# One change to an attention and two-layer network kernel: own raw buffers for the fourth head pair of the first group, and other engines allowed for casts, copies and scalings

## The chip, the cores and the metric

The kernel runs on one core of a Trainium2 chip. The metric is the device time of one execution in microseconds (us). The kernel before takes 654.95 us, the median of three runs (654.11 to 655.26). A core has five engines with a program each, that wait for one another by semaphores: TensorE (PE in the profile, its weight loads PEld), VectorE (DVE), ScalarE (ACT), GpSimd (POOL) and SyncE (SP), which here issues nearly all DMAs. An engine works off its program in order: whatever waits, holds up all that stands behind it on that engine.

## The reference

Attention over 4 batches of 8 heads, 768 positions and 64 numbers a head. A query sees the first 8 positions and the last 96 before it; scores are lowered by a slope times the distance. Its output, 3072 rows of 512, goes through a network of two layers:

```python
scores = scale * q @ k.T + bias           # bias = -slope[h] * distance
a = exp(scores - max) ; a = a / (sum(a) + 1e-9)
x = (a @ v) as (B*S, H*D)                 # 3072 x 512
h = x @ w_in                              # 512 x 2048
g = where(h > 0, h, exp(min(h, 0)) - 1)
out = g @ w_out                           # 2048 x 512
```

The weights come as 64-bit floats and the result must be nearly exact, so the two large products are each made of three: every factor is split into a high part (rounded to fp32r) and the rest, and high*high, high*low and low*high are summed.

## The kernel before, in words

**Tiling.** The 3072 rows are cut into 12 groups of 256 rows. In a group the 8 heads are handled as 4 pairs (two heads fill the 128 partitions). The hidden size of 2048 is cut into 16 chunks `fc` of 128, each with a tile of the first weights (`w0`) and of the second (`w1`).

**The stages.** Groups 0, 1 and 2 use the method of `pair` with `rows` set, and `pair32`: a pair's raw data is loaded into `rqv` (queries and values) and `rk` (keys), the queries are multiplied by the scale in place (`scaled`), PE makes the scores `s` (`s L691`), VectorE adds the distance table and takes the row's extreme (L647), ScalarE takes the exponential (L649), the sums are inverted on VectorE (L662, L663), the probabilities `pr` are multiplied by the inverse (`norm`; four tiles a pair), PE transposes them into `t` (L708), the transposed are copied out of PSUM into `pt`, and PE multiplies by the values into `pv` (L725). `pv` is copied as high part into `xh`, and the rest is subtracted. The copies, casts and subtractions of all stages go through the helpers `copy` and `minus`, so their lines in the profile are L336 (ScalarE), L338 (VectorE or GpSimd copies) and L344 (differences).

Beside that, `weight` turns each weight tile into two fp32r parts: a load of 512 KB (`bits`), four passes over 128x512 on ScalarE and VectorE (L433 to L442) that make an fp32 `g` of it, a cast of `g` to the high part, and a subtraction for the low part. The network for groups 0 to 2 (`moe`: `h L803`, `o L763`) runs over chunks 0 to 4 first, for all three groups, then 5 to 9, then 10 to 15. From group 3 on another scheme (`moe7`) with sums of weights (`combos`) takes over, with its TensorE order written out (`seq`).

**What sets the order.** Every operation is given to a planner with the engines that it may run on and a cost for each, with the tiles that it reads and writes and a due time. `Plan.order` then plays the program through with these costs and fixes for every operation the engine and the place in that engine's program; so a cost that is changed moves everything behind it. An alternative is a triple: engine, cost in ns, and whether it is held to take the port that VectorE and GpSimd share. Buffers are slots with names. The raw data of a pair in groups 0 to 2 lies in one of three slots (`rqv0`, `w015`, `w115`; keys `rk0`, `w014`, `w114`; the `w` names are space that the last weights use later). A pair's load thus waits until the pair three places earlier has finished its product with the values.

In `run` some weight loads are afterwards put together, right behind the load of the queries and values of group 1's second pair: those of the chunks named in `ASKED`. In the gaps that the planner foresees early on, `warm` and `fill_gap` put products that nobody reads (`none<-fill`, `o<-w 128x128`), which keep TensorE busy.

Of the kernel before, what the change touches and what calls it, by code (L numbers as in the profile page):

```python
# [16 lines left out]
P = 128  # L17
# [4 lines left out]
HK = WN // 2  # L22
NT = 2
W = NT * P
BIG = float(2 ** 100)

HI, LO = 0, 1
# [232 lines left out]
def act(n, psum=False, extra=0.0):  # L260
    return (("ACT", (55 if psum else 97) + 0.834 * n + extra, False),)


def dve(n, fast=False, port=False):
    return (("DVE", (75 + 0.521 * n) if fast else (70 + 1.042 * n), fast or port),)


def pool(n, two=True):
    return (("POOL", (30 + 2.58 * n) if two else (50 + 1.1 * n), True),)


def sp():
# [3 lines left out]
class Kernel:  # L276
# [136 lines left out]
    def weight(self, which, fc, due, after):  # L413
        nc, p, DM = self.nc, self.plan, self.DM
        tag = f"w{which}{fc}"
        bits = self.sb(tag, "bits", [P, 2 * DM], I32)
        g = self.sb("io", "g", [P, DM], I32)
        w = self.sb(tag, f"w{which}", [P, 2, DM], F32R)
        src = (self.w_in, self.w_out)[which][fc].bitcast(I32)
        words = lambda: bits.t.rearrange("p (n w) -> p n w", w=2)  # L420
        low, high = lambda: words()[:, :, 0], lambda: words()[:, :, 1]
        gf = lambda: g.t.bitcast(F32)

        def fetch(e):
            nc.sync.dma_start(bits.t, src)
            while self.values:
                self.values.pop(0)()

        load = p.add(sp(), fetch, writes=[bits], due=due - 9000, after=after, nbytes=P * DM * 8)
        if fc in self.ASKED:  # L430
            self.asked.append(load)
        if which in self.ABS:
            p.add((("ACT", 575.0, False),), lambda e: nc.scalar.activation(gf(), high().bitcast(F32), AF.Abs), [bits], [g], due - 6000)  # L433
            p.add(dve(DM, True), lambda e: nc.vector.tensor_scalar(gf(), gf(), F64_MIN, F64_MAX, ALU.max, ALU.min), [g], [g], due - 5500)
        else:
            p.add(dve(DM, port=True), lambda e: nc.vector.tensor_scalar(
                gf(), high().bitcast(F32), F64_MIN, F64_MAX, ALU.abs_max, ALU.min), [bits], [g], due - 5500)
        p.add(dve(DM, True), lambda e: nc.vector.tensor_scalar(g.t, g.t, 3, 0x3FFFFFFF, ALU.logical_shift_left, ALU.bitwise_and),
              [g], [g], due - 5000)
        p.add(dve(DM, port=True), lambda e: nc.vector.scalar_tensor_tensor(g.t, high(), -0x40000000, g.t, ALU.bitwise_and, ALU.bitwise_or),  # L440
              [bits, g], [g], due - 4500)
        p.add(dve(DM, port=True), lambda e: nc.vector.scalar_tensor_tensor(g.t, low(), 29, g.t, ALU.logical_shift_right, ALU.bitwise_or),  # L442
              [bits, g], [g], due - 4000)
        p.add(act(DM), lambda e: self.copy(e, w.t[:, HI], gf()), [g], [w], due - 3000)
        p.add((pool(DM) if due < 90000.0 else ()) + dve(DM, port=True), lambda e: self.minus(e, w.t[:, LO], gf(), w.t[:, HI]),
              [g, w], [w], due - 2000)
        if which == 0 or fc < self.NF7:
            cols = slice(0, DM) if which == 0 else slice(DM // 2, DM)
            self.stores[which, fc] = p.add(sp(), lambda e: nc.sync.dma_start(self.kept[which][fc], w.t.bitcast(F32)[:, :, cols]), [w],
                                           due=due + self.KEEP, nbytes=P * DM * 8 // (1 + which), floor=self.KEEP)  # L450
        return w
# [30 lines left out]
    def pair(self, b, gi, hp, xh, xl, due, ahead, step, X):  # L482
        nc, p = self.nc, self.plan
# [4 lines left out]
        rows = X.get("rows")  # L488
        nq, nk = W, KW
        rqv = self.sb("rqv", "rqv", [P, nq + VC if rows else nq], slots=X.get("rqv"))  # L490
        rv = rqv if rows else self.sb("rv", "rv", [P, VC])
        rk = self.sb("rk", "rk", [P, nk], slots=X.get("rk"))
        src = self.qkv[b, gi, hp]
        early = due - 9000 if rows else ahead - 9000
        if b == gi == 0 and hp < 3:

            vs, ks = slice(nq + P, nq + VC), slice(k0, nk)
# [26 lines left out]
        if rows:  # L524

            if "held" in X:
                self.loads += loads
            p.add((() if b == gi == 0 and hp < 3 else act(W) + dve(W, True)) + pool(W, False),
                  lambda e: self.scaled(e, q32(), q32(), sc), [rqv], [rqv], due - 9000)
            pv = self.bank("pv", "pv", [P, NT, P], X.get("pv"))  # L530
            self.pair32(b, hp, t0, q32, k32, v32, rqv, rk, pv, due, step, X)
            pvs = lambda: pv.t.rearrange("p i w -> p (i w)")
            p.add(act(W, True) + dve(W), lambda e: self.copy(e, xh.t[:, HI, hp], pvs()), [pv], [xh], due + 700)
            p.add(dve(W), lambda e: self.minus(e, xh.t[:, LO, hp], pvs(), xh.t[:, HI, hp]), [pv, xh], [xl], due + 800)
            if "held" in X:
                self.held += [o for v in (rqv, rk) for o in v.readers]
            return
# [139 lines left out]
    def pair32(self, b, hp, t0, q32, k32, v32, rqv, rk, pv, due, step, X):  # L677


        nc, p = self.nc, self.plan  # L680
# [5 lines left out]
        d = due - step  # L686
# [13 lines left out]
        for j in range(2):  # L700
            for i, x in enumerate(tiles):
                self.norm(prs[j][i], x[2], st, j * NT + i, d - 3000 + 2 * j + i, True)
            tp = self.bank("t", "t", [P, NT, 2, P], X.get("t"))

            def transposes(e, j=j, tp=tp):
                for i, (_, _, _, a0, kr, blocks) in enumerate(tiles):
                    for a in range(a0, 2):
                        nc.tensor.transpose(tp.t[:kr, i, a], prs[j][i].t[:, blocks[a]], self.ident.t)  # L708

            n = sum(2 - x[3] for x in tiles)  # L710
            p.add((("PE", 20 + 108.0 * n, False),), transposes, prs[j], [tp], d - 2500 + j)
            pt = self.sb("pt", "pt", [P, NT, 2, P], slots=X.get("pt"))
            pts.append(pt)
            if t0:
                p.add(act(NT * 2 * P, True) + dve(NT * 2 * P), lambda e, pt=pt, tp=tp: self.copy(e, pt.t[:HK], tp.t[:HK]), [tp], [pt], d - 2000 + j)
            else:
                for i, (_, _, _, a0, kr, _) in enumerate(tiles):
                    p.add(act((2 - a0) * P, True) + dve((2 - a0) * P), lambda e, pt=pt, tp=tp, i=i, a0=a0, kr=kr: self.copy(
                        e, pt.t[:kr, i, a0:], tp.t[:kr, i, a0:]), [tp], [pt], d - 2000 + j)

        def values(e):
# [213 lines left out]
    def build(self):  # L935
# [11 lines left out]
        for n, f0, f1 in segs:  # L947
            start.setdefault(n, at)
            d, at0 = {}, at
# [11 lines left out]
        for n, (b, gi) in enumerate(groups):  # L961
# [6 lines left out]
            for hp in range(self.NP):  # L968
                d = lo + (hp + 1) * (hi - lo) / self.NP
                X_ = self.EARLY[min(n, len(self.EARLY) - 1)]  # L970
                if n > self.GS:
                    X_ = {"seven": True}
                ahead = last - 2500
                if n > self.GS:
                    ahead = start[self.GS] + self.PERIOD * (4 * (n - self.GS - 1) + hp - 2) + self.VISIT
# [40 lines left out]
    AFTER = 2 * PERIOD  # L1016
    PASSES, SINCE = 2, 195000.0
    GS, KEEP, COMBO = 3, 100000.0, 0.0
    LATE, ASKED = 11, (2, 3, 4)
    ABS = (0, 1)  # L1020
    LINE = 32
    PLACE = {"w015": (80, 0), "w014": (0, 48), "w012": (80, 0), "w013": (0, 48), "xh0": (160, 0), "xh1": (32, 0), "gg0": (80, 0), "gg1": (0, 0)}
# [293 lines left out]
```

## Time and profile before

| What | us |
|---|---|
| median of three runs | 654.95 |
| the profiled execution | 655.49 |
| its span, first to last instruction | 653.70 |
| TensorE busy in the span | 642.0 (98%) |
| VectorE busy | 522.0 (80%) |
| ScalarE busy | 478.4 (73%) |
| GpSimd busy | 27.1 (4%) |

The profiled execution is one run; its span leaves out 1.8 us around the program. Busy time of TensorE counts also the products that nobody reads, and each product's modelled end reaches into the next one. In the chain of waits, each piece is what the end of the program hung on at that time, followed backwards.

### The profile page before, as it was taken

To read this page: it belongs to the slowest core of one execution; us is meant where nothing else is said; L and a number is where in the kernel's file an instruction comes from. 1 tells how busy PE (TensorE), PEld (TensorE's weight loads), DVE (VectorE), ACT (ScalarE), POOL (GpSimd) and SP (SyncE) were. 2 spreads that over 40 slices of the span, in tenths; PEclk is the share of its full clock that TensorE was granted. 3 is DMA by queue.
4 is the path that set the end of the run, shared out by engine and by line. 5 is a ranking of instruction groups with operands and counts; after the bars stand their busy time and mean duration, and the time that the engine had idled before them with its cause. 6 is when DMAs were issued, how large, how long until landed. Compare 5 with 4: busy or idle time off the path is not lost.

```text
span 653.7 us, 15985 instructions
## 1 busy us (share of the span) xinstructions
PE 642.0 (98%) x5950; PEld 599.4 (92%) x5950; DVE 522.0 (80%) x1520; ACT 478.4 (73%) x1244; POOL 27.1 (4%) x54
## 2 busy tenths in 40 slices
PE   8899999999999999999999999999999999999996
PEld 6677888888888999999999999999999999999996
DVE  7999999999999867866877886876777778766655
ACT  6898888765778777776777777776777777774442
POOL 3152100000000000000000000000000000000000
PEclk9999999999999999999999999999999999999999
DMA  8835996810237567667756756766775675574661
GB/s 273 293 118 193 383 379 223 301 61 17 71 114 255 198 212 255 224 196 224 264 187 214 272 180 221 253 218 202 230 262 181 223 282 189 178 255 169 209 211 36
DMA packets 52373, 137.71 MB, mean 211 GB/s; under 512 B 5698, under 2 KB 19010, under 8 KB 52290
## 3 DMA queue, kind: packets, MB, share of 16 engines
q1 hardware_dynamic: 52000, 136.37, 61.6%
q8 instruction: 48, 0.79, 0.5%
q14 instruction: 35, 0.29, 0.1%
q10 hardware_dynamic: 290, 0.26, 0.1%
HBM read 119.84 MB, written 16.78 MB: 209 GB/s over the span
## 4 chain that ended last, share of the span: by engine, by line
PE 90%; DVE 4%; ACT 2%; DMA 2%; issue 1%; POOL 0%; DVEq 0%; POOLq 0%; SPq 0%
PE h L803 39%; PE a L880 26%; PE o L763 9%; PE pv L614 4%; PE s L556 3%; PE t L576 3%; PE s L691 2%; DMA rqv<-in_qkv_dram 2%; PE pv L725 2%; PE t L708 2%; ACT pr L649 1%; DVE g L464 1%; PE none L1084 0%; DVE gl L344 0%; ACT pt L336 0%
## 5 line engine op out<-in xcount | busy, mean ns | idle before, releaser
L803 PE MATMUL h<-xh,w0s 128*128 128x256 f32 x1728 | 203.1, 276 | 0.0
L803 PEld LDWEIGHTS h<-xh,w0s 128*128 128x128 f32 x1728 | 199.5, 188 | 0.1
L880 PE MATMUL a<-w,gg 128*128 128x256 f32 x864 | 143.7, 277 | 0.3 <-DVE xh L344 0.3
L336 ACT CAST gg<-z 128x384 fp32r<-128x384 f32 (+1 forms) x144 | 81.4, 566 | 69.7 <-DVE z L735 29.7
L735 DVE SCALAR_TENSOR_TENSOR z<-z,h 128x512 f32<-128x512 f32 x72 | 49.5, 688 | 92.9 <-ACT z L734 86.0
L880 PEld LDWEIGHTS a<-w,gg 128*128 128x128 f32 x864 | 120.4, 188 | 0.6 <-DVE xh L344 0.5
L649 ACT ACTIVATE pr<-pr,nmax 128x232 f32<-128x232 f32 (+1 forms) x192 | 90.0, 471 | 9.2 <-DVE nmax L647 8.9
L344 DVE TENSOR_TENSOR gg<-z,gg 128x512 fp32r<-128x512 f32 (+1 forms) x144 | 84.9, 618 | 7.2 <-ACT gg L336 6.6
L803 PEld LDWEIGHTS h<-xh,w 128*128 128x128 f32 x576 | 81.7, 188 | 8.8 <-issue 1.1
L803 PE MATMUL h<-xh,w 128*128 128x256 f32 x576 | 86.7, 282 | 0.1
L835 DVE TENSOR_TENSOR z<-z 128x128 f32<-128x128 f32 (+1 forms) x216 | 72.0, 333 | 5.2
L880 PE MATMUL a<-ta,gg 128*128 128x256 f32 x432 | 72.2, 276 | 0.0
L647 DVE CUSTOM_DVE_ANT_0 pr<-s,tab 128x232 f32<-128x232 f32 (+1 forms) x192 | 63.5, 374 | 5.6 <-PE s L556 5.6
L733 ACT ACTIVATE z<-h 128x512 f32<-128x512 f32 x72 | 43.0, 597 | 33.2 <-PE h L803 32.9
L763 PE MATMUL o<-w,gh 128*128 128x512 f32 x192 | 59.8, 403 | 0.8 <-ACT gh L336 0.4
L880 PEld LDWEIGHTS a<-ta,gg 128*128 128x128 f32 x432 | 59.6, 188 | 0.0
L880 PE MATMUL a<-tb,gg 128*128 128x256 f32 x216 | 50.0, 294 | 0.0
L734 ACT ACTIVATE z<-z 128x512 f32<-128x512 f32 x72 | 45.5, 632 | 1.8
L633 ACT ACTIVATE pr<-pr,st 128x232 f32<-128x232 f32 (+1 forms) x90 | 38.9, 469 | 9.6 <-DVE st L669 7.3
L880 PEld LDWEIGHTS a<-tb,gg 128*128 128x128 f32 x216 | 34.4, 188 | 3.8 <-issue 0.2
L763 PEld LDWEIGHTS o<-w,gh 128*128 128x128 f32 x192 | 31.8, 188 | 5.8 <-ACT gh L336 1.1
L649 ACT ACTIVATION_READ_ACCUMULATOR pr<-pr,nmax 128x1 f32 x192 | 36.8, 192 | 0.0
(126 smaller groups left out, 916.4 us busy)
## 6 DMA issues: line engine op xcount, KB each, us to landing
w0s<-kept SPq DMA_DIRECT2D x144, 512.0 KB, 5.0
rk<-in_qkv_dram SPq DMA_DIRECT2D x45, 184.0 KB, 2.8
bits<-in_w_in_dram SPq DMA_DIRECT2D x16, 512.0 KB, 6.5
bits<-in_w_out_dram SPq DMA_DIRECT2D x16, 512.0 KB, 9.4
kept<-w SPq DMA_DIRECT2D x16, 512.0 KB, 4.4
rv<-in_qkv_dram SPq DMA_DIRECT2D x32, 256.0 KB, 3.6
rqv<-in_qkv_dram SPq DMA_DIRECT2D x13, 384.0 KB, 3.5
rqv<-in_qkv_dram SPq DMA_DIRECT2D x34, 128.0 KB, 3.8
```

Of the source, the lines that this page charges most:

```text
L336: self.nc.scalar.copy(out, x)
L344: self.on(e).tensor_tensor(out, x, y, ALU.subtract)
L633: self.nc.scalar.activation(out, x, AF.Copy, scale=sc)
L647: p.add((("DVE", 158 + 1.042 * n, False),), lambda e: nc.vector.tensor_tensor_reduce(pr.t[:, lo:], st_()[:, lo:], tab, -(2.0 ** -(h + 1)), ...
L649: p.add(act(n, extra=200), lambda e: nc.scalar.activation(pr.t[:, lo:], pr.t[:, lo:], AF.Exp, bias=nm, scale=-1.0, accum_out=st.t[:, 0, i: ...
L733: p.add(act(n, True), lambda e: nc.scalar.activation(out(), hx(), AF.Relu, scale=-1.0), [h], [ex], due)
L734: p.add(act(n), lambda e: nc.scalar.activation(out(), out(), AF.Exp, scale=-1.0), [ex], [ex], due)
L735: p.add(dve(n), lambda e: nc.vector.scalar_tensor_tensor(out(), out(), -1.0, hx(), ALU.add, ALU.max), [h, ex], [ex], due)
L763: nc.tensor.matmul(acc[i].t, g.t[:, i * P:(i + 1) * P], w2.t[:, s], start=fc == f0 and n == 0 and s == HI, stop=fc == f1 - 1 and n == 1)
L803: self.nc.tensor.matmul(hx(), w1.t[:, s, cc * P:(cc + 1) * P], xh.t[:, x, cc], start=n == 0 and cc == 0, stop=n == 2 and cc == self.NCC - 1)
L835: tt = lambda e, out, x, y, op: self.on(e).tensor_tensor(out, x, y, op)
L880: nc.tensor.matmul(of[i].t[:, j], gg.t[:, x, g], w(s), start=first and x == s == 0 and (n in (0, 2, 4, 6) or final and n == 5), stop=last ...
```

## The change

There are five edits. The fourth pair of the first group gets raw buffers of its own (`ks0` for queries and values, `qs0` for keys, space that later stages use), and its loads get a later due time (25000 where 11000 stood). Of the weight loads that `run` puts together only chunk 2's stay (`ASKED`). The cast of a weight's high part may go to GpSimd. The copies of the transposed probabilities in groups 0 to 3 may go to ScalarE alone (before also to VectorE), and the scaling of the queries of all but the first three pairs to ScalarE or GpSimd (before also to VectorE). And GpSimd's costs for operations with one input are others, and those are no longer held to take the shared port.

```diff
 def pool(n, two=True):
-    return (("POOL", (30 + 2.58 * n) if two else (50 + 1.1 * n), True),)
+    return (("POOL", (30 + 2.58 * n) if two else (30 + 1.85 * n), two),)
+
+
+def cast(n):
+    return (("POOL", 50 + 1.14 * n, False),)
...
-        p.add(act(DM), lambda e: self.copy(e, w.t[:, HI], gf()), [g], [w], due - 3000)
+        p.add(act(DM) + cast(DM), lambda e: self.copy(e, w.t[:, HI], gf()), [g], [w], due - 3000)
...
-        early = due - 9000 if rows else ahead - 9000
+        early = X.get("asked", due - 9000) if rows else ahead - 9000
...
-            p.add((() if b == gi == 0 and hp < 3 else act(W) + dve(W, True)) + pool(W, False),
+            p.add((() if b == gi == 0 and hp < 3 else act(W)) + pool(W, False),
                   lambda e: self.scaled(e, q32(), q32(), sc), [rqv], [rqv], due - 9000)
...
-                p.add(act(NT * 2 * P, True) + dve(NT * 2 * P), lambda e, pt=pt, tp=tp: self.copy(e, pt.t[:HK], tp.t[:HK]), [tp], [pt], d - 2000 + j)
+                p.add(act(NT * 2 * P, True), lambda e, pt=pt, tp=tp: self.copy(e, pt.t[:HK], tp.t[:HK]), [tp], [pt], d - 2000 + j)
...
-                    p.add(act((2 - a0) * P, True) + dve((2 - a0) * P), lambda e, pt=pt, tp=tp, i=i, a0=a0, kr=kr: self.copy(
+                    p.add(act((2 - a0) * P, True), lambda e, pt=pt, tp=tp, i=i, a0=a0, kr=kr: self.copy(
...
+                if n == 0 and hp == 3:
+                    X_ = dict(X_, rqv=["ks0"], rk=["qs0"], asked=25000.0)
...
-    LATE, ASKED = 11, (2, 3, 4)
+    LATE, ASKED = 11, (2,)
```

Counted over the whole program, 20 of the 32 casts of weights move from ScalarE to GpSimd; 8 copies of transposed probabilities move from VectorE to ScalarE; of the scalings of queries 6 leave VectorE and 1 leaves ScalarE, all to GpSimd; of the products of probabilities with the inverse sum 9 more go to VectorE, 4 fewer to ScalarE and 5 fewer to GpSimd; and one `gl` difference goes from GpSimd to VectorE.

SyncE's program at its start, before. `rqv_302` and `rk_201` are the raw data of group 0's fourth pair, `rqv_348` and `rk_213` of group 1's first, `rqv_390` and `rk_234` of its second; `bits` are weights.

```order
L425 DMA bits_186<-in_w_in_dram 128x1024
L425 DMA bits_188<-in_w_out_dram 128x1024
L425 DMA bits_191<-in_w_out_dram 128x1024
L517 DMA rk_201<-in_qkv_dram 128x368
L517 DMA rk_213<-in_qkv_dram 128x368
L517 DMA rk_234<-in_qkv_dram 128x368
L516 DMA rqv_302<-in_qkv_dram 128x768
L516 DMA rqv_348<-in_qkv_dram 128x768
L517 DMA rk_371<-in_qkv_dram 128x368
L516 DMA rqv_390<-in_qkv_dram 128x768
```

The same place now, where the fourth pair's data are `rqv_188` and `rk_191`, and those of group 1's first two pairs `rqv_303`, `rk_195` and `rqv_351`, `rk_220`:

```order
L429 DMA bits_186<-in_w_in_dram 128x1024
L520 DMA rqv_188<-in_qkv_dram 128x768
L521 DMA rk_191<-in_qkv_dram 128x368
L521 DMA rk_195<-in_qkv_dram 128x368
L429 DMA bits_209<-in_w_out_dram 128x1024
L429 DMA bits_214<-in_w_out_dram 128x1024
L521 DMA rk_220<-in_qkv_dram 128x368
L521 DMA rk_238<-in_qkv_dram 128x368
L520 DMA rqv_303<-in_qkv_dram 128x768
L520 DMA rqv_351<-in_qkv_dram 128x768
```

The fourth pair's loads moved ahead of two weight loads and no longer stand behind a buffer that must come free; the loads of group 1's first two pairs have moved up one place in the ring of three slots.

TensorE's program before, from the transposes of the second pair (`t_296`, `t_304`) on; `pv_330` is that pair's product with the values:

```order
L708 MATMUL t_296<-ident,pr_215 128x128
L708 MATMUL t_296<-ident,pr_218 116x128 x2
L708 MATMUL t_304<-ident,pr_228 128x128
L708 MATMUL t_304<-ident,pr_230 116x128 x2
L1084 MATMUL none<-fill 128x512 x4
L725 MATMUL pv_330<-pt_310,rqv_165 64x128
L725 MATMUL pv_330<-pt_316,rqv_165 64x128
```

And now, where the second pair's transposes are `t_299` and `t_308`, and `s_313`, `s_314` are the fourth pair's scores:

```order
L712 MATMUL t_299<-ident,pr_217 128x128
L712 MATMUL t_299<-ident,pr_222 116x128 x2
L712 MATMUL t_308<-ident,pr_232 128x128
L712 MATMUL t_308<-ident,pr_235 116x128 x2
L695 MATMUL s_313<-rk_191,rqv_188 128x128
L695 MATMUL s_314<-rk_191,rqv_188 128x128
L695 MATMUL s_313<-rk_191,rqv_188 128x232
L695 MATMUL s_314<-rk_191,rqv_188 128x232
L1090 MATMUL none<-fill 128x512
```

The fourth pair's scores, which before stood behind the third pair's transposes, now stand in front of the second pair's product with the values, in the place of three of four products that nobody reads.

GpSimd's program before, at the products of probabilities with the inverse sums of the second (`pr_215`, `pr_218`), third (`pr_262`, `pr_275`) and fourth pair (`pr_381` to `pr_404`) and the next one:

```order
L637 TENSOR_SCALAR pr_215<-pr_215,st_226 128x128
L637 TENSOR_SCALAR pr_218<-pr_218,st_226 128x232
L637 TENSOR_SCALAR pr_262<-pr_262,st_267 128x128
L637 TENSOR_SCALAR pr_275<-pr_275,st_267 128x128
L637 TENSOR_SCALAR pr_381<-pr_381,st_385 128x128
L637 TENSOR_SCALAR pr_387<-pr_387,st_385 128x128
L637 TENSOR_SCALAR pr_404<-pr_404,st_385 128x232
L637 TENSOR_SCALAR pr_426<-pr_426,st_445 128x232
```

And now (`pr_232` is the second pair's, `pr_264` and `pr_294` the third's, `pr_328` and `pr_371` the fourth's):

```order
L641 TENSOR_SCALAR rqv_188<-rqv_188,scale 128x256
L641 TENSOR_SCALAR pr_232<-pr_232,st_230 128x128
L342 CAST w_99_330<-g_242 128x512
L641 TENSOR_SCALAR pr_264<-pr_264,st_291 128x128
L641 TENSOR_SCALAR pr_294<-pr_294,st_291 128x128
L641 TENSOR_SCALAR rqv_303<-rqv_303,scale 128x256
L641 TENSOR_SCALAR rqv_351<-rqv_351,scale 128x256
L641 TENSOR_SCALAR pr_328<-pr_328,st_342 128x128
L641 TENSOR_SCALAR pr_371<-pr_371,st_342 128x232
L342 CAST w_105_468<-g_373 128x512
L348 TENSOR_TENSOR w_105_468<-g_373,w_105_468 128x512
```

Scalings of queries and casts of weights now stand between the products with the inverse sums; those of the fourth pair stand behind the scalings of two pairs of group 1. From the first transposes of the later scheme (L576) on, TensorE's programs are the same row for row.

## Rows read from the trace of the kernel before

**Rows 1.** Page, its head.

```profile
span 653.7 us, 15985 instructions
```

**Rows 2.** Busy time by engine in four stretches: PE, PEld, DVE, ACT, POOL; clock, DMA, GB/s.

```profile
0.00:10.00 10.00, 8.45 (x35) 6.70 (x36) 7.18 (x46) 5.24 (x17) 3.68 (x15) 1.00 0.77 243
10.00:62.00 52.00, 47.81 (x381) 36.62 (x380) 49.66 (x170) 46.52 (x148) 16.20 (x25) 1.00 0.61 206
62.00:197.00 135.00, 134.35 (x934) 116.98 (x932) 131.53 (x349) 103.92 (x283) 7.18 (x15) 1.00 0.54 198
197.00:654.00 457.00, 451.41 (x4606) 439.13 (x4604) 333.60 (x958) 322.71 (x799) 0.00 (x0) 1.00 0.64 214
```

**Rows 3.** The chain that ended last, 10 to 62 us: start, us, what.

```profile
19.52 4.09 DMA rqv<-in_qkv_dram
...
23.63 0.51 ACT rqv L633
...
26.72 0.47 ACT w L336
...
33.68 0.30 ACT gh L336
...
46.73 3.60 DMA rqv<-in_qkv_dram
...
50.35 0.35 DVE rqv L635
...
57.22 0.35 DVE rqv L635
```

**Rows 4.** Timeline, SyncE and TensorE, 13 to 27 us: start, us, engine, line, operation.

```profile
13.01 0.33 SPq L516 DMA_DIRECT2D rqv<-in_qkv_dram  x1
...
13.67 0.76 PE L708 MATMUL t<-ident,pr 128*116 128x128 f32 x5 [0.47 <-POOL pr L637]
...
17.31 0.89 PE L691 MATMUL s<-rk,rqv 64*128 64x128 f32 x8
...
26.87 1.07 PE L803 MATMUL h<-xh,w 128*128 128x256 f32 x4
```

**Rows 5.** VectorE's groups by shape, 0 to 62 us: busy, mean ns, idle before.

```profile
L635 DVE TENSOR_SCALAR pr<-pr,st 128x232 f32<-128x232 f32 x8 | 3.0, 392 | 0.0
L635 DVE TENSOR_SCALAR rqv<-rqv,scale 128x256 f32<-128x256 f32 x5 | 2.5, 503 | 0.3 <-DMA rqv<-in_qkv_dram 0.3
...
L338 DVE COPY pt<-t 116x512 f32<-116x512 f32 x2 | 1.4, 678 | 0.0
...
L338 DVE COPY pt<-t 116x256 f32<-116x256 f32 x2 | 0.8, 425 | 0.2 <-ACT pt L336 0.2
```

**Rows 6.** ScalarE's groups by shape, 0 to 62 us.

```profile
L336 ACT CAST w<-g 128x512 fp32r<-128x512 f32 x9 | 5.6, 618 | 0.0
L336 ACT COPY pt<-t 116x512 f32<-116x512 f32 x9 | 5.2, 577 | 0.3 <-PE t L708 0.2
L633 ACT ACTIVATE pr<-pr,st 128x232 f32<-128x232 f32 x11 | 5.2, 489 | 1.2 <-DVE st L663 1.2
```

**Rows 7.** GpSimd's groups by shape, 0 to 62 us.

```profile
L637 POOL TENSOR_SCALAR pr<-pr,st 128x232 f32<-128x232 f32 x13 | 7.1, 553 | 21.3 <-DVE st L663 17.4 <-ACT w L336 4.0
L344 POOL TENSOR_TENSOR w<-g,w 128x512 fp32r<-128x512 f32 x4 | 5.2, 1296 | 3.2 <-ACT w L336 3.0
...
L637 POOL TENSOR_SCALAR rqv<-rqv,scale 128x256 f32<-128x256 f32 x5 | 2.4, 482 | 4.2 <-DMA rqv<-in_qkv_dram 3.4 <-DVE n_six L401 0.8
```

**Rows 8.** Timeline, GpSimd and VectorE side by side, near 12.5 and 43 us.

```profile
12.18 1.44 POOL L637 TENSOR_SCALAR pr<-pr,st 128x128 f32<-128x128 f32 x2 [2.35 <-DVE st L663]
...
12.69 0.68 DVE L440 SCALAR_TENSOR_TENSOR g<-bits,g 128x512 int32<-128x512 int32 x1
...
42.89 1.27 POOL L344 TENSOR_TENSOR w<-g,w 128x512 fp32r<-128x512 f32 x1
...
43.23 1.09 DVE L635 TENSOR_SCALAR rqv<-rqv,scale 128x256 f32<-128x256 f32 x1
```

## The prediction, made before the result was known

> **What bounds the kernel now.** I read the busy times by stretch first, to see where TensorE can gain at all. From 62 to 197 us it is busy 134.35 of 135 us, and from 197 us on only the tail leaves gaps [rows 2]; its program is the same row for row from the later scheme's first transposes on. In those stretches the sum of TensorE's work is the time, and the change takes no useful product away. Before 62 us it is different: TensorE is busy 8.45 of 10 and 47.81 of 52 us, and part of that are products that nobody reads [rows 2]. So the gain or loss is made in the first 62 of 653.7 us [rows 1].
>
> The second view is the chain of waits in that time. It hangs on other engines in turn: on the load of raw data at 19.52 (4.09 us), on ScalarE from 23.63 to 33.98, then for 12.7 us on TensorE itself, on another load at 46.73 (3.60 us), on VectorE from 50.35 to at least 57.57 [rows 3]. The third view, the busy times again, shows why: between 10 and 62 us VectorE is busy 49.66 of 52 us and ScalarE 46.52, GpSimd only 16.20 [rows 2]. The stretch is bound by VectorE and ScalarE nearly alike, with the ring of three raw buffers in between.
>
> **The sum, part by part.** The profiled execution took 655.49 us, 0.54 above the median of the runs shown, with a span of 653.7 and 1.8 around it; differences are made against it and put on the median.
>
> *The fourth pair's own buffers.* Before, its queries and values were asked for at 13.01, when the first pair's product with the values had freed a slot, and its scores began at 17.31 [rows 4]. Now eleven loads stand ahead of it, one of them on ScalarE's queue: three each of 131, 135 and 197 KB and two weights of 524 KB, together 2.4 MB, and 3.0 MB with its own two. At 243 GB/s [rows 2] they have landed at 12.4 us, with the 1 us of the start 13.4. The scaling takes 0.48 [rows 7]. The place in TensorE's program comes up when the second pair's transposes end, before at 13.67 + 0.76 = 14.43 [rows 4]. So the scores can begin 2.8 us earlier. The two loads that freed-up places bring forward are those of group 1's first two pairs: the one at 19.52 in the chain waited for the third pair's product and now waits for the second's, about one pair's work earlier, 2 to 3 us.
>
> Part of it is given back. On GpSimd two of the fourth pair's products with the inverse sums now stand behind the scaling of `rqv_351`. Its load leaves when the second pair's product is done, at about 16.5, lands up to 4.09 later [rows 3], and after two more small operations and the scaling the products end near 21.9; without that queue they could have ended nearer 20.6. I take 1.5 us of the 2.8 as lasting. Ends: 0.5 (the queue takes nearly all) and 2.8.
>
> *ScalarE.* I count its program up to its eighth first pass over `h` (L733), which before falls near the stretch's end. It loses 9 of 11 casts of weights at 0.618 = 5.6 us [rows 6], two scalings at 0.51 = 1.0 [rows 3] and two products with the inverse at 0.489 = 1.0 [rows 6]. It gains two copies of 116x512 at 0.577 = 1.2 [rows 6] and five smaller operations, taken at 0.4 each, 2.0. Net 4.4 us less, or 9.5% of its 46.5 busy us [rows 2]. The chain hangs on it for 10.3 us [rows 3], so 1.0 us. Bounds: nothing, if those 10 us turn out to be waits for others, and 1.7, if two casts and a scaling that stand in the stretch go (0.5 + 2 x 0.6).
>
> *VectorE.* Counted to the twelfth pair's last table addition: five scalings at 0.503 and five copies (two at 0.678, two at 0.425, one smaller) go, 5.1 us; six products with the inverse at 0.392, one smaller and one pass over a weight come, 3.4 [rows 5]. Net 1.7 less, 3.4% of 49.66; on the 7.2 us of the chain that is 0.2 to 0.3, and I take 0.3. If by luck the 1.09 us scaling at 43.23, which sat beside a difference on GpSimd [rows 8], finds no successor, up to 0.7 more.
>
> *GpSimd.* Eight of the ten first weights' casts come to it and eight scalings. No row shows a cast there. A one-input operation of half the size takes 0.482, a two-input one of full size 1.296 [rows 7]; these are the ends. I take 0.72, nearer to the one-input row, since a cast reads one tensor. The load, 8 x 0.72 + 8 x 0.48 less two or three products, is some 8 us on top of 16.2 of 52 [rows 2]; as a sum it hides. What it may do to VectorE is not shown for casts; beside one-input operations the row shows no delay: 0.68 for L440 at 12.69, its usual time, while the two GpSimd operations at its side took 1.44 us [rows 8] where smaller ones take half that. Two operations of that kind at 0.553 [rows 7] would be 1.1. So I put 0.2 us on the chain, bounds 0 and 1.6 (8 x 0.2, all of it felt).
>
> *The rest.* The four weight loads that `ASKED` no longer gathers stay in the same queue a few places later, among loads; DMA is 61% busy there [rows 2], which covers them; without cover each is late by one raw load. The later due time only fixes the queue's order, counted above. One product more that nobody reads and five fewer small ones stand in TensorE's idle time. After 62 us the twelve further casts leave ScalarE, which has 31 us to spare there [rows 2], and TensorE's 0.65 idle us are all that could be won or, if a weight came late, be the first to grow.
>
> Sum: -1.5 - 1.0 - 0.3 + 0.2 = -2.6 us. On the profiled execution 655.49 - 2.6 = 652.9, on the median 654.95 - 2.6 = 652.3.
>
> By the Trainium skill, "SBUF — State Buffer", section "Who interferes with whom", VectorE and GpSimd share one pair of ports as an exclusive lock: whichever starts first holds it for its whole instruction, and the other blocks, where VectorE reads two tensors or uses both its ports. The trace agrees that one of the two is stopped (the 1.09 us scaling beside a two-input GpSimd difference [rows 8]), but beside one-input operations GpSimd was the one to wait. By the rule with GpSimd first, the term above would be the 5.8 us of the third rival.
>
> **Rivals.**
>
> *Nothing that can be measured (0.2% is 1.3 us).* VectorE is busy 95% of the stretch [rows 2]. An earlier fourth pair then only changes the order in which the same work is done, and the 1.7 us that it loses is eaten by 8 x 0.2 us beside the casts. Against it: the chain hangs on VectorE for only 7.2 of these 52 us. Time 654.9.
>
> *Slower by GpSimd's queue.* GpSimd now scales the queries of nearly every pair of groups 1 and 2, and a scaling waits for its load, with products, casts and differences of weights behind it. Before, GpSimd waited 21.3 us for inverse sums with nothing else behind [rows 7], so the wait cost nothing. If at four of the eight places a product or a cast that TensorE waits for comes 1.2 us later (a scaling of 0.48 and most of a cast), 4.8 - 2.6 = +2.2 us, 657.1. It decides from two such places on. For it: the fourth pair's products already stand so. Against: the loads of these pairs come up to a pair earlier.
>
> *Slower by the shared port.* Each of the eight casts, when it begins first, stops VectorE for its 0.72 us: 5.8 us on the engine that is 95% busy, 5.8 - 2.6 = +3.2, 658.1. It decides from four casts on. For it is the scaling of 1.09 us, against it the 0.68 of L440 [rows 8].
>
> *More.* The whole 2.8 us last, ScalarE gives 1.7 and VectorE 0.4: -4.9, 650.0.
>
> **How the numbers follow.** My forecast has a chance of 0.55 (own range 651.0 to 653.6), "more" 0.08, "nothing" 0.20, GpSimd's queue 0.10, the port 0.07. Faster by over 0.2%: 0.55 + 0.08 = 0.63; within: 0.20; slower: 0.17. The range for the time is 650.0 to 656.2: from the best sum to the end of "nothing" (654.95 + 1.3), which leaves out the two slower rivals.
>
> **What would show it.** The fourth pair's scores (the fourth group of eight `s L691` products) begin at 14 to 15 us instead of 17.31, and the first `h L803` at 25 to 26 instead of 26.87 [rows 4]. The chain's load at 19.52 begins before 18. ScalarE's busy time between 10 and 60 us falls by some 4 us, and casts on GpSimd take 0.6 to 0.9. The first transposes L576, at 197.2 before (where the fourth stretch of [rows 2] begins), come 2 to 3 us earlier, and everything from there on takes as long as before. I am wrong if VectorE's instructions beside the casts are longer than their usual means [rows 5], if TensorE waits for GpSimd in more places than before, or if waits appear after 62 us, which I have counted as closed.

## The result, and the profile after

The changed kernel takes 663.86 us (median of 4 runs, 663.54 to 664.71) against 655.11 of the kernel before beside it: a ratio of 1.0136, interval 1.0124 to 1.0148, some 8.8 us slower. The forecast was 652.3. The profiled execution took 664.11 us, 8.62 more than the 655.49 of before. Lines of the changed kernel stand 4 (further down 6) below those of before: L691 is now L695, L576 is L580.

The page's head, which answers to [rows 1]:

```profile
span 662.3 us, 15996 instructions
```

The same four stretches as in [rows 2], the third ended at the later scheme's first transposes, now at 199.8:

```profile
0.00:10.00 10.00, 8.49 (x38) 6.79 (x39) 7.43 (x48) 5.33 (x18) 3.41 (x14) 1.00 0.78 244
10.00:62.00 52.00, 46.07 (x384) 35.37 (x384) 49.81 (x165) 43.41 (x142) 25.98 (x36) 1.00 0.62 210
62.00:199.80 137.80, 136.35 (x930) 117.62 (x925) 134.92 (x351) 99.40 (x277) 20.37 (x26) 1.00 0.53 194
199.80:662.30 462.50, 456.69 (x4605) 444.51 (x4604) 332.32 (x954) 321.11 (x794) 0.00 (x0) 1.00 0.64 211
```

There are two losses. The first transposes come 2.6 us later (199.8 for 197.2). From there on the kernel needs 462.5 us instead of 653.7 - 197.2 = 456.5, or 6.0 more, though TensorE's program there is the same row for row and its granted clock 1.00 in both. Between 10 and 62 us VectorE is as busy as before (49.81 of 52 us) although by the prediction's count 1.7 us of work had been taken from it, and TensorE is busy for 1.7 us less.

The first loss by groups, 0 to 62 us, to be held against [rows 5] and [rows 7]. VectorE:

```profile
L639 DVE TENSOR_SCALAR pr<-pr,st 128x232 f32<-128x232 f32 (+1 forms) x14 | 5.5, 418 | 0.0
L438 DVE TENSOR_SCALAR g<-g 128x512 f32<-128x512 f32 x10 | 5.3, 538 | 0.0
L442 DVE TENSOR_SCALAR g<-g 128x512 int32<-128x512 int32 x10 | 4.8, 500 | 0.1
...
L666 DVE TENSOR_SCALAR st<-st 128x4 f32<-128x4 f32 x10 | 3.3, 325 | 0.2 <-ACT pr L653 0.2
```

Before, the same two operations on `g`:

```profile
L434 DVE TENSOR_SCALAR g<-g 128x512 f32<-128x512 f32 x10 | 4.3, 432 | 0.3 <-ACT g L433 0.3
L438 DVE TENSOR_SCALAR g<-g 128x512 int32<-128x512 int32 x10 | 4.1, 423 | 0.1
```

Their means go from 432 and 423 ns to 538 and 500. GpSimd in the same time, now:

```profile
L641 POOL TENSOR_SCALAR pr<-pr,st 128x232 f32<-128x232 f32 (+1 forms) x16 | 9.4, 596 | 8.3 <-DVE st L667 2.9 <-ACT pr L653 2.6 <-ACT e L737 2.0
L641 POOL TENSOR_SCALAR rqv<-rqv,scale 128x256 f32<-128x256 f32 x12 | 8.2, 684 | 16.6 <-DMA rqv<-in_qkv_dram 11.5 <-PE t L712 3.5 <-DVE n_six L405 0.9
L342 POOL CAST w<-g 128x512 fp32r<-128x512 f32 x8 | 5.8, 722 | 6.7 <-DVE g L446 6.7
```

A cast takes the 0.72 us that I had put in. But the scaling of `rqv` went from 482 [rows 7] to 684 ns on the mean; the chain below has one of 1.15 us. In the timeline, the first three rows are TensorE's start of the fourth pair's scores, of the next pair's and of the first pass over `h` [rows 4]; the last three show a cast on GpSimd meeting VectorE:

```profile
13.71 0.89 PE L695 MATMUL s<-rk,rqv 64*128 64x128 f32 x8
...
19.15 1.05 PE L695 MATMUL s<-rk,rqv 64*128 64x232 f32 x8 [1.54 <-POOL rqv L641]
...
27.21 0.84 PE L807 MATMUL h<-xh,w 128*128 128x256 f32 x4
...
42.99 0.41 DVE L442 TENSOR_SCALAR g<-g 128x512 int32<-128x512 int32 x1
...
43.20 0.67 POOL L342 CAST w<-g 128x512 fp32r<-128x512 f32 x1 [1.55 <-DVE g L446]
...
43.33 0.83 DVE L438 TENSOR_SCALAR g<-g 128x512 f32<-128x512 f32 x1
```

The cast begins at 43.20, the scaling at 43.33 takes 0.83 us, twice its 0.41. By the Trainium skill, "SBUF — State Buffer", section "Who interferes with whom", VectorE and GpSimd share a pair of ports as an exclusive lock, held for a whole instruction. The trace agrees in direction: here, with GpSimd first, 0.54 us of the cast were left, and VectorE's scaling took 0.42 us longer, not the whole 0.54.

TensorE's waits between 10 and 62 us show where it surfaces, on GpSimd's results above all. First the one row on GpSimd of before (total us, times, longest), then the three longest now:

```profile
PE t L708 <- POOL pr L637: 0.8, 2, 0.5
...
PE s L695 <- POOL rqv L641: 2.0, 2, 1.5
PE t L712 <- POOL pr L641: 1.5, 3, 0.7
PE t L712 <- ACT pr L637: 1.0, 1, 1.0
```

The chain of waits shows both losses. Its first rows answer to [rows 3]: the load that began at 19.52 now begins at 15.91, but from 20 to 46 us the chain hangs on VectorE nearly alone. The last two rows show the second loss; they are one and the same piece of TensorE's program, 48 products of 256 columns, in two neighbouring stretches:

```profile
15.91 3.75 DMA rqv<-in_qkv_dram
...
23.89 0.75 DVE g L438
24.64 1.17 DVE st L666
...
43.41 0.75 DVE g L438
...
46.99 1.15 POOL rqv L641
...
56.16 3.23 DMA rqv<-in_qkv_dram
...
446.77 5.65 PE h L807 x48
...
460.61 5.44 PE h L807 x48
```

5.65 / 48 = 118 ns for a product, or 5.44 / 48 = 113. I looked at all 32 runs of feed-forward products between two visits of the attention after the first transposes. Each keeps one pace from its tenth product at the latest to its end, and by it the stretches can be written down, S for 118 ns and a point for 113:

```
before                   ........S...........S..........S..
after                    ...S.S......SSSSSSSS....SSSSSSS.S.
```

Of the 32, 17 are slow instead of 3: 14 x 0.38 us (0.21 on the 48 products, 0.17 on the 42 around them) = 5.3 us. The one or two signs behind the 32nd stand for the beginning and the rest of the run of some 400 products after the last visit. That run does not keep one pace: in the changed kernel its first 110 products or so are slow and the rest fast, which costs 0.5 us more (46.9 us busy for 46.4). Together that is 5.8 of the 6.0 us.

### The profile page after: what moved, and what is told of

It is laid out like the page before. It is cut to its first block, busy times and chain, and to the rows that moved or that the text cites. A ratio compares the mean times of both kernels' runs of the same rounds, so it can differ in the third digit from the quotient of the medians.

```text
span 662.3 us, 15996 instructions
## 1 busy us (share of the span) xinstructions
PE 647.6 (98%) x5946; PEld 604.3 (91%) x5946; DVE 524.5 (79%) x1516; ACT 469.3 (71%) x1227; POOL 49.8 (8%) x75
## 4 chain that ended last, share of the span: by engine, by line
PE 78%; DVE 13%; ACT 4%; DMA 2%; issue 1%; POOL 1%; SPq 1%; DVEq 0%; POOLq 0%; ACTq 0%
PE h L807 34%; PE a L884 26%; PE o L767 5%; PE pv L618 4%; PE s L560 3%; PE t L580 3%; DMA rqv<-in_qkv_dram 2%; DVE pr L651 1%; DVE g L444 1%; DVE g L446 1%; DVE w L348 1%; DVE g L438 1%; DVE gl L348 1%; ACT pr L653 1%; PE s L695 1%
## 5 line engine op out<-in xcount | busy, mean ns | idle before, releaser
L807 PE MATMUL h<-xh,w0s 128*128 128x256 f32 x1728 | 206.4, 279 | 0.0
L807 PEld LDWEIGHTS h<-xh,w0s 128*128 128x128 f32 x1728 | 202.8, 188 | 0.1
L807 PE MATMUL h<-xh,w 128*128 128x256 f32 x576 | 88.6, 283 | 0.7 <-DVE e L739 0.7
L637 ACT ACTIVATE pr<-pr,st 128x232 f32<-128x232 f32 (+1 forms) x86 | 37.2, 470 | 9.3 <-DVE st L673 7.1
L340 ACT COPY pt<-t 128x128 f32<-128x128 f32 (+2 forms) x88 | 37.3, 437 | 4.9 <-PE t L712 3.6
```

The lines of the kernel that those rows point to most:

```text
L340: self.nc.scalar.copy(out, x)
L637: self.nc.scalar.activation(out, x, AF.Copy, scale=sc)
L807: self.nc.tensor.matmul(hx(), w1.t[:, s, cc * P:(cc + 1) * P], xh.t[:, x, cc], start=n == 0 and cc == 0, stop=n == 2 and cc == self.NCC - 1)
```

## Experiments

Theory 1 for the second loss: tile addresses. A slot gets its SBUF address by the order of first use. The fourth pair now uses `ks0` and `qs0` (3072 and 2048 bytes a partition) before the probabilities, so `pr`, `pt`, `xh`, `gg` lie 5,120 bytes further up (and two slots of weights of equal size, `w03` and `w12`, change places). Rival: the time or the order of events. Theory 2 for the first: GpSimd's casts stop VectorE. Rivals: GpSimd's queue, or weights that come late.

In "places of before" the slots are touched once, in the order of the kernel before, ahead of the work (`OLD` stands for that list); no instruction is added:

```diff
-            f.run()
+            [(f.w if s[0] == "w" else f.m).tile([P, 32], F32, tag=s, name=f"first_{s}") for s in OLD.split()]; f.run()
```

**Places exchanged** (e1: changed kernel with OLD; e2: kernel before with the changed kernel's list).

> The changed kernel, its program unaltered, but every tile at the SBUF address that it had before the change: the slots are touched in the old order ahead of the work. In the changed kernel the fourth pair's slots ks0 and qs0 are first used earlier, and so xh, gg, pr and pt lie 5,120 bytes further up. Theory 1 (the places decide): the first transposes of the later scheme stay at about 199.8, but from there on TensorE is back at 113.3 ns for a 256-column product, the rest takes 456.5 us instead of 462.5, total about 657.8. Rival (the pace is set by when things happen, by the chip or by the order): it stays slow for about 240 us, total about 663.9.

> The kernel before, its program unaltered, but every tile at the address that it has in the changed kernel. Theory 1 (the places decide): first transposes at about 197.2, from there on some 240 us at 118 ns per 256-column product, 462 us instead of 456.5, total about 661. Rival: 655.0, unchanged.

Measured: e1 659.90 us, ratio 1.0062 (1.0039 to 1.0086); e2 660.98, 1.0087 (1.0061 to 1.0112). The stretch after the first transposes, in e1:

```profile
201.40:658.90 457.50, 451.53 (x4605) 439.43 (x4604) 332.66 (x956) 320.83 (x794) 0.00 (x0) 1.00 0.64 214
```

and in e2:

```profile
197.30:659.10 461.80, 456.47 (x4605) 444.25 (x4604) 333.42 (x957) 322.77 (x799) 0.00 (x0) 1.00 0.65 212
```

457.5 and 461.8 us: the second loss goes and comes with the addresses. Theory 1 holds. e1's total is 2 above what was expected, because its first transposes came at 201.4 and not 199.8. That delay begins early, on GpSimd:

```profile
13.13 0.98 POOL L641 TENSOR_SCALAR rqv<-rqv,scale 128x256 f32<-128x256 f32 x1 [3.81 <-DMA rqv<-in_qkv_dram]
14.10 0.87 POOL L641 TENSOR_SCALAR pr<-pr,st 128x128 f32<-128x128 f32 x1
```

The fourth pair's load was awaited until 13.13 (in the changed kernel until 11.91), and the second pair's product with the inverse sums stands behind its scaling; so the second pair's transposes went on at 15.03 instead of 13.23. That is the rival of GpSimd's queue at work. Why the load came later there, no run shows. The patterns, with those of all later runs that bear on them:

```
e1 after, old places     ........S...........S..........S..
e3 casts on ScalarE      ........S...........S..........S..
e4 own buffers alone     ........S...........S..........S..
e6 no cast, no own       ........S...........S..........S..
e5 casts alone           .S......S...........S..........S..
e9 idle casts            .S......S...........S..........S..
e2 before, new places    ...S.S......SSSSSSSS....SSSSSSS.S.
e7 xh and gg moved       .SSSSSSS....S.SSSSSS....S.SSSSS.S.
e8 gg moved              .SSSSSSS....SSSSSSSS....SSSSSSS.S.
e10 gg0 by 320 bytes     .SSSSSSSSSSSSSSSSSSSSSSSSSSSSSSSS
e11 ks, qs, pr, pt moved ..SSSSS.....SSSSSSS.....SSSSSSS.S.
e14 all by 64 bytes      ................................S.
e15 all by 256 bytes     ........S...........S..........S..
```

Kernels with different work in the first 200 us, but the same addresses, have the same pattern in the 32 (two of them with one stretch more); kernels with the same program and other addresses do not, unless all tiles move by 256 bytes. In the run after the last visit the addresses do not settle it alone: in e1, e3, e4 and e15 about 90 of its products are slow, in e6 none of them.

**Which tiles** (e7, e8, e11: `ks0 qs0` put elsewhere in OLD; e10 as below).

```diff
-e7:  "... st2 io1 xh0 ..."                 e8:  "... xh1 gg0 ..."
+e7:  "... st2 io1 ks0 qs0 xh0 ..."         e8:  "... xh1 ks0 qs0 gg0 ..."
+e11: "... ks0 qs0 pr1 ... gl2 pt0 pr0 ..."
-e10: "gg0": (80, 0)
+e10: "gg0": (0, 80)
```

> The kernel before, program unaltered; ks0 and qs0 lie ahead of xh0, so that xh and gg lie 5,120 bytes further up, as in the changed kernel, while the probabilities pr and their transposes pt stay. If the addresses of what the feed-forward products read make the pace (xh moving and gg stationary): about half of the 256-column products at 118 ns after the first transposes, total 660 to 661. Rival (those of the attention's tiles pr and pt, whose products stand just ahead of each stretch): 655.8.

> The kernel before, program unaltered; ks0 and qs0 lie ahead of gg0, so that of the tiles that the feed-forward products read only two of the three slots of gg lie 5,120 bytes further up. If gg decides: 660 to 661 as with both moved. If xh decides, or pr and pt: 655.8.

> The kernel before, program unaltered; only the first of the two gg slots is moved, by 320 bytes down within its place, and all else stays where it was. If a gg slot's place by itself makes the pace: slow blocks in the third of the feed-forward stretches that read it at least, total 657 to 661. Rival (in the run before it was the distance of 5,120 bytes, or that ks0 and qs0 were moved too, and 320 bytes do nothing): 655.8.

> The kernel before, program unaltered; ks0 and qs0 lie where the changed kernel has them, and pt0 and pr0 go to the end in their place, so that xh and all slots of gg keep their addresses. If gg's place alone decides: 655.8, about a tenth of the 256-column products at 118 ns. Rival (the place of ks and qs, whose scores stand just ahead of each stretch, or of pr and pt): 660 to 662, half of them at 118.

Measured: e7 661.91 (1.0096, 1.0080 to 1.0113), e8 661.03 (1.0089, 1.0070 to 1.0109), e10 667.44 (1.0187, 1.0170 to 1.0204), e11 661.03 (1.0087, 1.0070 to 1.0104). In e10 (its slow products start every 118 to 120 ns) the chain shows, where the changed kernel had its fast stretch:

```profile
461.11 5.65 PE h L803 x48
```

So 320 bytes on one slot cost 11.9 us, more than the 657 to 661 in all that I had expected. But "gg alone" fell: e11 leaves every `gg` where it was, and 19 of its 32 stretches are slow. The places of several tiles count; which, and in what combination, is open.

**All tiles together** (e14, e15: an unused tile of 64 or 256 bytes ahead of both pools).

```diff
+            f.w.tile([P, 16], F32, tag="wpad", name="first_pad")   # e15: 64 instead of 16
```

> The kernel before, program unaltered; every tile of the two working pools lies 64 bytes further up, by an unused tile of that size ahead of them, so that all distances between them are kept. If the distances between tiles set the pace: the same three slow stretches (ninth, twenty-first and thirty-second) and 655.6. Rival (absolute addresses): another set of slow stretches, total 654 to 667.

> The same with 256 bytes. If distances set the pace: the same three slow stretches, 655.6. If absolute addresses do, but only within some small unit: one of the two paddings alters the set and the other not.

Measured: e14 654.71 (0.9983, 0.9973 to 0.9993), e15 656.00 (1.0004, 0.9994 to 1.0013). With all distances kept, 64 bytes alter the pattern and 256 do not. So the distances alone don't decide; that 256 bytes do nothing would fit a unit that divides 256, which two paddings don't prove. Nor can such a unit be all: the 5,120 bytes of e2 are 20 x 256, and there the distances changed. In e14 none of the 32 is slow, only the beginning of the run after them, and it is the only version here that beats both kernels, by 1.0 us of 655.7.

**Parts of the change, at the places of before** (e3: all but the casts; e4: own buffers and order of loads alone, e12 the same once more; e5: casts alone; e6: the remaining edits).

```diff
 e3: -act(DM) + cast(DM)   +act(DM)        # L448; the rest as changed
 e4: +rqv=["ks0"], rk=["qs0"], asked=25000.0   +ASKED (2,)   # the rest as before
 e5: -act(DM)   +act(DM) + cast(DM)        # the rest as before
 e6: +act alone for pt, act or pool for rqv, pool's new cost   # the rest as before
```

> The changed kernel without the casts on GpSimd (ScalarE alone casts the weights, as before), all other edits kept, tiles at the addresses of before. Theory 2 (GpSimd's casts lengthen VectorE's and their own neighbours' operations, and that is the loss before 200 us): VectorE's scalings of g are back at 430 ns from 538, first transposes at 196.5 or earlier, total 654 to 655. Rival (GpSimd's queue with the scalings of q, or the copies all on ScalarE): first transposes stay at 199 to 200, total 657 to 658.

> The kernel before with the fourth pair's own buffers and the order of the loads (two of the five edits) alone, tiles at the addresses of before. As the prediction had it: scores of the fourth pair at 14 to 15, first transposes 1.5 us earlier, at 195.7, total 653.5. Rival (VectorE bounds the stretch, an earlier fourth pair wins nothing): 197.2 and 655.0. A second rival (it delays the other raw pairs): 198 to 199, total 656 to 657.

> The kernel before with one edit, the weights' casts also allowed on GpSimd, tiles at the addresses of before. Theory 2 (GpSimd's casts stop VectorE's scalings of g beside them, which took 825 ns instead of 415 in the changed kernel): first transposes 2 to 4 us later than 197.2, total 657.5 to 660. Rival (the casts hurt only together with GpSimd's scalings of q, whose queue then is full): 197.2 and 655.8.

> The kernel before with the three remaining edits: copies of the probabilities on ScalarE alone, q scaled on ScalarE or GpSimd, and the planner's lower cost of GpSimd's one-input operations; no casts there, no own buffers, tiles at the addresses of before. If the parts add up, the run with own buffers alone (+3.4 on the median) and the one with all but the casts (0.0) leave -3.4 for these: first transposes at 194, total 652.4. Rival (the own buffers' runs only scattered, the parts are worth little each): 655 to 656.

> The own buffers alone once more, for a trace of one of its slower executions, which the first trace (655.96, clock 0.998) was not. If TensorE's clock makes their scatter: at a mean clock of 0.991 to 0.995 a stretch of some microseconds at half the clock within the first 62 us, and first transposes at 199 or later. Rival (late loads): clock 0.998 and TensorE idle for DMA.

Measured: e3 655.84 (1.0001, 0.9987 to 1.0015); e4 659.17 (1.0053, 1.0034 to 1.0071); e5 664.41 (1.0131, 1.0109 to 1.0154); e6 656.28 (1.0016, 1.0001 to 1.0031); e12, one execution, 656.50. Without the casts the rest of the change shows neither gain nor loss on the median; with them (e1) it is 4.1 us slower. The scalings of `g` (L434) in e3 are back at 416 ns on the mean, as Theory 2 had it, but its first transposes came at 198.5, not 196.5. The traced execution is one of e3's slower ones (657.19, where the ten reach from 654.38 to 658.11): TensorE's granted clock was 0.88, 0.50 and 0.77 in the three stretches of 2 us from 14 to 20. How much e3 would gain without that is not shown. The medians of e4 (+3.4) and e6 (+0.7) do not add up to e3 (0.0). Each part alters the planner's whole order, and, as shown next, the clock makes these medians scatter.

Own buffers alone do bring the fourth pair forward. e4's timeline, TensorE:

```profile
12.27 0.89 PE L691 MATMUL s<-rk,rqv 64*128 64x128 f32 x8 [1.21 <-POOL rqv L637]
...
18.11 1.05 PE L691 MATMUL s<-rk,rqv 64*128 64x232 f32 x8 [0.49 <-DVE rqv L635]
...
25.84 1.20 PE L803 MATMUL h<-xh,w 128*128 128x256 f32 x8
```

The scores start 5.0 us earlier than in [rows 4], the first pass over `h` 1.0 us earlier. Yet the first transposes are at 197.1 (e12: 198.3), as before: the lead is used up in the next stretch, where e4's chain runs through two raw loads almost end to end, between them one scaling, the scores and the product with the values:

```profile
35.12 3.41 DMA rqv<-in_qkv_dram
...
38.68 0.49 POOL rqv L637
...
39.21 1.05 PE s L691 x8
40.27 1.05 PE pv L725 x16
...
41.37 3.87 DMA rqv<-in_qkv_dram
```

The scatter of e4's ten timed runs goes with the mean granted clock: 655.9 us at 0.998, 657.0 and 658.5 at 0.997, 659.4 at 0.994, 661.5 at 0.991. Both its traces have 0.998 or more, so a typical execution of e4 was not traced; e12, run to catch one at a low clock, did not. What a low clock looks like is in e6, busy times of two microseconds each:

```profile
14.00:16.00 2.00, 1.37 (x12) 0.96 (x12) 1.89 (x4) 2.00 (x9) 0.00 (x0) 1.00 0.56 211
16.00:18.00 2.00, 0.74 (x8) 0.53 (x8) 1.97 (x8) 1.83 (x6) 0.84 (x2) 0.97 0.65 192
18.00:20.00 2.00, 2.00 (x10) 1.68 (x9) 2.00 (x12) 0.73 (x4) 0.48 (x1) 0.50 0.30 82
20.00:22.00 2.00, 2.00 (x16) 1.28 (x14) 1.23 (x4) 2.00 (x9) 0.00 (x0) 0.68 0.10 29
```

TensorE was busy 1.37 and 0.74 of 2 us, then ran at 0.50, that is 1.2 GHz, until about 21. e6's first transposes came at 199.6 in this execution. e5 has it too (first transposes 205.6), which is why its loss of 8.9 us is no measure of the casts alone:

```profile
10.00:62.00 52.00, 44.70 (x348) 34.85 (x347) 47.98 (x158) 39.68 (x128) 17.29 (x26) 0.93 0.55 185
```

**What a cast does by itself** (e9: an idle cast on GpSimd beside each of ScalarE's first ten; e13: 8 columns cast and the tile set to zero instead).

```diff
-lambda e: self.copy(e, w.t[:, HI], gf())
+lambda e: (self.copy(e, w.t[:, HI], gf()), due < 75000.0 and nc.gpsimd.tensor_copy(self.spare, gf()))
+# e13: tensor_copy(self.spare[:, :8], gf()[:, :8]), then memset(self.spare, 0.0)
```

> The kernel before, tiles at their places, with one addition: beside each of the first ten weights' casts, which stay on ScalarE, GpSimd casts the same tile g into a spare tile that nobody reads. So VectorE has what GpSimd's casts do to it, but no product waits for a cast on GpSimd (the products with the inverse sums behind one in GpSimd's queue may). Theory 2 (the shared access stops VectorE): some of the scalings of g at 800 ns and more, first transposes 2 to 5 us after 197.2, total 657.5 to 661. Rival (the casts hurt because the weights come late, by GpSimd's queue and its slower cast): 197 to 198, total 655.5 to 656.5.

> As the run with idle casts, but in each one's place GpSimd casts 8 columns of g (so it waits for the same tile) and then sets the spare tile to zero, which reads nothing. GpSimd's queue is as busy and stands in the same order. If VectorE's stop beside the casts is the loss: no scaling of g above 600 ns beside them, first transposes at 197 to 198.5, total 655.5 to 657. Rival (the place in GpSimd's queue is the loss: products and differences behind it come late): 200 to 201, total 659 to 660.

Measured: e9 659.54 (1.0063, 1.0047 to 1.0080), first transposes at 200.6; e13 656.09 (1.0009, 0.9994 to 1.0023), 197.7. No product waits for e9's casts, and yet they cost 3.4 us before the transposes. That is clear of the scatter: the kernel before at eight sets of addresses (before, e2, e7, e8, e10, e11, e14, e15) has its first transposes between 195.9 and 197.3. In e9's timeline a scaling of `g` takes 0.82 us beside a cast, another 1.51 beside a difference:

```profile
35.49 1.40 POOL L444 CAST spare<-g 128x512 fp32r<-128x512 f32 x2
...
35.59 0.82 DVE L434 TENSOR_SCALAR g<-g 128x512 f32<-128x512 f32 x1
...
37.97 1.54 POOL L344 TENSOR_TENSOR w<-g,w 128x512 fp32r<-128x512 f32 x1 [1.08 <-ACT w L336]
...
38.28 1.51 DVE L434 TENSOR_SCALAR g<-g 128x512 f32<-128x512 f32 x1
```

In e13 GpSimd was busy even longer with what stood in their place, 8.4 us (groups, 0 to 75 us) for 6.6 in e9:

```profile
L444 POOL MEMSET spare<- 128x512 f32 x10 | 5.8, 581 | 0.6
...
L444 POOL CAST spare<-g 128x8 fp32r<-128x8 f32 x10 | 2.6, 260 | 12.2 <-DVE g L442 9.4 <-DVE st L662 2.7
```

so a full queue by itself is not e9's loss. But a memset, too, stops VectorE, against my expectation that no scaling of `g` would take more than 600 ns beside one:

```profile
36.79 0.62 POOL L444 MEMSET spare<- 128x512 f32 x1
...
36.86 0.82 DVE L438 TENSOR_SCALAR g<-g 128x512 int32<-128x512 int32 x1
```

So e13 is no run without stops; it has fewer. I summed VectorE's stops up to 75 us: of each operation that lies beside one on GpSimd, its time less the median of its shape with nothing beside it, from 0.04 us up.

```
                 VectorE's stops, us                       first transposes
before           3.66 (differences 2.35, rest 1.31)        197.2
after            5.92 (casts 2.16, differences 1.20,       199.8
                 rqv 1.16, pr 1.40)
e9 idle casts    6.83 (casts 1.76, differences 4.15)       200.6
e13 memsets      3.30 (memsets 1.13, differences 1.12)     197.7
e2 before, new   3.33                                      197.3
```

Against before, stops and delay are +2.26 and +2.6 us (after), +3.17 and +3.4 (e9), -0.36 and +0.5 (e13). So they go together in these runs, within 0.9 us, but not in all: e1 has fewer stops than the changed kernel (some 5.4 us), and its transposes come 1.6 us later, by the load shown above. Part of e9's is indirect: behind a cast, GpSimd's differences fall beside other work of VectorE than before. That share is luck of the order; e13 doesn't separate it from the casts' own 1.76.

## Why the prediction was wrong

*From 62 us on "counted as closed", "everything from there on takes as long as before".* This step failed most: 6.0 of the 8.6 us. I argued from the instructions, which are the same. Their operands' addresses are not, and e1 and e2 show that these make the difference: 457.5 us with the old ones, 461.8 with the new. The kernel even has a table of hand-set offsets for `gg`, `xh` and some weights (PLACE), a sign that addresses count, which I read past. This term stood at nothing in the sum.

*GpSimd beside VectorE, +0.2 us (bounds 0 and 1.6).* VectorE's stops grew by 2.26 us. The row that I leaned on, 0.68 us for L440 beside a GpSimd scaling [rows 8], was one meeting in which VectorE took its usual time and GpSimd was held up. Where the cast was already running, a scaling of `g` took up to 0.42 us longer; the six stops beside casts made 2.16. The third rival had the mechanism, at a price too high: 5.8 us, as if each of eight casts met something and stopped it for its whole time. I gave it 0.07.

*Own buffers, -1.5.* The scores began at 13.71, even before the "14 to 15" named, and the load in the chain at 15.91, before 18, as foreseen. Nothing of it lasted: the first pass over `h` came at 27.21, not 25 to 26, and in e4, alone, the lead is gone by 197 us. That "an earlier fourth pair only changes the order in which the same work is done" stood in the rival "nothing", and it is what happened.

*ScalarE, -1.0, and VectorE, -0.3.* ScalarE's busy time fell by 3.1 us between 10 and 62 (46.52 to 43.41), nearly the 4 expected. But the chain left ScalarE for VectorE, so it won nothing. VectorE's 1.7 us less of work were eaten by the 2.26 us more of stops (counted up to 75 us): 49.66 us busy before, 49.81 after.

*GpSimd's queue.* TensorE waited for GpSimd 3.5 us in five places, where I had given the slower rival 0.10. e13 shows that a fuller queue by itself costs 0.5 us at most, but it held no added scaling of `rqv`. e1 shows one such place: a late load held up the second pair's product behind the scaling, and its transposes went on 1.8 us later than in the changed kernel. What the 2.6 us of the changed kernel owe to such waits and what to the stops is open.

Without the casts and with the old addresses the change gives 655.84, ratio 1.0001 (e3): what is left is the rival "nothing", as far as runs between 654.38 and 658.11 can tell.

## What to carry to other kernels

When a change alters which buffer is used first, compare the addresses of the tiles before calling any later stretch unchanged; an identical program is not an identical time. An operation moved to GpSimd can lengthen VectorE's beside it (here 0.83 us for 0.41), so it need be no gain while VectorE bounds the stretch, and one meeting in a trace does not tell what the others will cost. A lead at the start lasts only if the next resource in the chain has room for it.

## What the hardware showed unexpectedly

With the granted clock at 1.00, products of 256 columns started every 113 or every 118 ns, and a stretch of 90 of them kept the pace that it had by its tenth. The addresses of the tiles decide: 3 slow stretches of 32 in the kernel before, 17 with tiles 5,120 bytes further up, all but the first with one slot moved by 320 bytes (+11.9 us), none with all moved by 64 (-1.0 us), again the same three with all moved by 256. By the kernel's lists of slots, the `h` products from group 4 on read `xh` from one of two places and the weights from a ring of four, and both fast and slow stretches use them within one execution; so no pair of places by itself does it. That it is settled where a stretch begins is a guess from the pace being kept; the run after the last visit changes its pace on the way. How it comes about is not shown.
